# Loading V in one transfer, and U and V behind the first batch's last chunk

## The chip, the cores and the metric

The kernel runs on one core of one Trainium2 chip. The metric is the device time of one execution in microseconds (us); lower is better. The times of the kernel before are three executions.

## What is computed

For each of 4 batches and 8 heads, 768 positions of width 48 go through a recurrent attention; its result `x` (768 x 384 for each batch) goes through a low-rank mixing over the positions and a two-layer MLP:

```
for t in range(S):
    cur = einsum('bhd,bhe->bhde', u[None] * kt, vt)
    y[:, :, t] = einsum('bhd,bhde->bhe', rt, state + cur)
    state = w[None, :, :, None] * state + einsum('bhd,bhe->bhde', kt, vt)
...
h = xt @ U @ V                      # U is 768 x 32, V is 32 x 768
u = x + h.transpose(0, 2, 1)
out = u + maximum(u @ w_ch1, 0) @ w_ch2     # 384 -> 1536 -> 384
```

U, V and the MLP's weights arrive as 64-bit floats. The kernel reads them as pairs of 32-bit integers and makes 32-bit floats of them on ScalarE and VectorE.

## The kernel before, in words

Each batch is cut into 6 chunks of 128 positions (`NCH`). For a chunk `n` three tensors are loaded (`a_load`, L732: k, r and v, in this order, 192 KB each in 1,024 rows of 192 bytes). The first batch's chunks 0 to 5 make up the front of the kernel. In the front GpSimd (POOL) makes three products of each chunk (`a_ks`, L783 and L786; `a_dv`, L798; `a_dv_u`, L811), VectorE (DVE) reduces the last one (`a_dg`, L818), scales and copies the transposed r (`a_tr`, L858), masks the scores (`a_am`, L1018), adds states (L1059) and forms `x` (`a_x`, L1027). TensorE (PE) transposes k and r (L849), makes scores (L881), state updates (L895), and the chunk's output (`a_visit`, L914 and L918). ScalarE (ACT) scales v (L822) and decays the state (L1067).

U is used in `g_product` (L1132): for each chunk six matmuls multiply its `x` by U. V is spread to three copies on partitions by a selection matrix `sel` (`v_split`: four matmuls for each half, seen as L414 writing `pab`), and its high and low parts are kept in `V3` (L670, L671). When all six chunks have their product, `c_g` writes `Gs` (L1156 to L1164), `c_xu` adds V times `Gs` to the transposed `x`, and the first batch's MLP begins. PE then works through the MLP of one batch after another, with the attention of the next batch woven in. All matmuls of the helper `whole` carry line 414.

Every operation is first recorded with a key. A planner in the kernel (`Plan.schedule`) goes through them with costs of its own, gives each to an engine, and writes one fixed order for each engine; the engines then take their instructions strictly in that order. Of the operations that an engine could begin, the smaller key goes first. A product or subtraction that either engine can do (`on_either`) goes to POOL or to DVE, and DVE and POOL take turns in those that use their shared port; the planner writes these turns down as waits. A load has a planned landing time (`LANDS`, and `late` for each load). SyncE's queue (SP) issues nearly all loads.

The keys that matter here: chunk `n` of the front loads at `-90 + n`, so chunk 4 at -86 and chunk 5 at -85. U's load has key -86.5 and V's -85.5. U's conversion has key 16 (`U_CONV`), V's 30.05 (`LATER`), chunk c's output `9 + 4.2 * c`. The first four MLP weights load behind the third chunk's scores in the plan, which for SP is only a place in the order.

```
at(t_load, load)         # U: -86.5, V: -85.5
for n in range(1, NCH):
    at(-90 + n, lambda n=n: a_load(n))
```

So SP issues: chunks 0 to 3, U, chunk 4, V in four parts, chunk 5, weights. The parts of V are the four column blocks of 192 columns: part c fills partitions 32c to 32c + 31.

Of the kernel before, what the change touches and what calls it, by code (L numbers as in the profile page):

```python
# [341 lines left out]
def dve(n):  # L342
    return 130 + 1.09 * n


def act(n):
    return 285 + 0.6 * n
# [7 lines left out]
def rwkv_moe(ctx: ExitStack, tc: tile.TileContext, r, k, v, w, u, U, V, w1, w2, out):  # L355
# [11 lines left out]
    R = U.shape[1]  # L367
# [26 lines left out]
    def wbuf(shape, dt, tag, bufs, name):  # L394
        return Buf(work, shape, dt, tag, bufs, name)
# [7 lines left out]
    def bank(tag, name):  # L403
        if tag in lasting:
            return lasting[tag]
        return Buf(ps, [128, 512], F32, tag, {"acc": 3}.get(tag, 1), name)

    def f32(ap):
        return ap.bitcast(F32)


    def whole(*args, **kw):

        return nc.tensor.matmul(*args, **kw)  # L414
# [7 lines left out]
    def on_act(n, fn, w_, r_, times=1, dk=0.0):  # L422
        return op("ACT", times * (act(n) - 94) + 94, fn, w_, r_, dk=dk)

    def on_either(n, fn, w_, r_, dk=0.0, only=None):

        ways = [("POOL", pool(n), lambda: fn(nc.gpsimd), True), ("DVE", dve(n), lambda: fn(nc.vector), True)]
        return one_of(ways, w_, r_, only, dk)
# [5 lines left out]
    def dma(fn, w_, r_, rows, run, eng="SP", ns=470, dk=0.0, late=0.0, either=False):  # L434

        q = nc.scalar if eng == "ACT" else nc.sync
        return op(eng, ns, lambda: fn(q), w_, r_, dma=rows * max(0.96 if run >= 500 else 1.18 if run == 192 else 1.3, run / 366),
                  rows=rows, late=late, dk=dk, alt=[("ACT", ns, lambda: fn(nc.scalar), False)] if either else ())
# [9 lines left out]
    ident_ = const.tile([128, 128], F32, name="ident")  # L448
# [27 lines left out]
    sel = wbuf([128, 3 * 128], F32, "xh", NXS, "sel")  # L476
# [87 lines left out]
    def big(shape, dt, name):  # L564
        return xbuf(shape, dt, "big", NBIG, name)
# [6 lines left out]
    def unit(name, shape, parts, split):  # L572

        P_ = shape[0]
        n = 1
        for s_ in shape[1:]:
            n *= s_
        raw = big([128, 2 * n], I32, f"raw_{name}") if wide else big([128, n], F32, f"raw_{name}")

        def view(ap):  # L580
            return ap if len(shape) == 2 else ap.rearrange("p (a c) -> p a c", a=shape[1])

        loaded = [(raw, i) for i in range(len(parts))]

        def load(mark=None):
            big_one = len(parts) == 1 and name != "u"
            before = landing[-FLYING] if big_one and len(landing) >= FLYING else None
            mine = []
            if big_one:
                landing.append((mine, Buf(const, [1, 1], F32, None, 1, f"landed_{name}")))  # L590
            for i, (p0, ap) in enumerate(parts):
                runs = 1 if len(ap.shape) == 2 else ap.shape[1]

                def start(q, p0=p0, ap=ap):
                    mine.append(q.dma_start(view(raw.t[p0:p0 + ap.shape[0]]), ap.bitcast(I32) if wide else ap))  # L595
                    if before:
                        tc.add_manual_dep(mine[0].ins, before[0][0].ins.name,
                                          mybir.DependencyInfo(mybir.DependencyClass.Sync, mybir.DependencyReason.DATA),
                                          reason="no more of them at a time")
                dma(start, [(raw, i)] + ([landing[-1][1]] if big_one else []), ([before[1]] if before else []) + ([mark] if mark else []),  # L600
                    ap.shape[0] * runs, (8 if wide else 4) * n // runs, ns=370, late=LATE + 1500 * (name == "v") + SLACK * (big_one and len(landing) <= 2 * EARLY))

        def word(i):
            return raw.t[:P_].rearrange("p (n two) -> p two n", two=2)[:, i]

        def byte():
            return raw.t[:P_].bitcast(U8).rearrange("p (n e) -> p n e", e=8)[:, :, 3]

        def fl():
            return view(word(0).bitcast(F32) if wide else raw.t[:P_])  # L610

        def on_dve_byte():
            return nc.vector.tensor_scalar(word(0), byte(), 2.0 ** -5, 7.0, ALU.mult, ALU.min)

        def on_act_byte():

            nc.scalar.activation(word(0), byte(), AF.Copy, scale=7.49 / 255)  # L620

        def sign():
            return nc.vector.scalar_tensor_tensor(word(0), word(1), -2 ** 31, word(0), ALU.bitwise_and, ALU.bitwise_or)

        def join():
            return nc.vector.scalar_tensor_tensor(word(0), word(1), 3, word(0), ALU.logical_shift_left, ALU.bitwise_or)  # L626

        def convert():
            if wide:
                op("DVE", 100 + 0.65 * n, on_dve_byte, [(raw, "lo")], loaded, lock=True,  # L630
                   alt=[("ACT", act(n) + 100, on_act_byte, False)])
            if wide:
                on_act(n, lambda: nc.scalar.activation(word(1).bitcast(F32), word(1).bitcast(F32), AF.Copy,  # L633
                                                       scale=2.0 ** -112), [(raw, "hi")], loaded)
                mark = [pool_done] if name in ALONE else []
                op("DVE", dve(n), sign, [(raw, "lo")], [(raw, "hi")] + mark, lock=True)
                op("DVE", dve(n), join, [(raw, "lo")], [(raw, "hi")], lock=True)
            split(fl, raw)
        return load, convert

    def weight_units():
        units = []

        def split_to(d, key, name):
            t = d[key] = big([128, 2, DM], F32R, name)

            def go(fl, raw):
                def to(i):
                    return t.t[:, i] if len(fl().shape) == 2 else t.t[:, i].rearrange("p (c n) -> p c n", c=NCT)
                on_act(384, lambda: nc.scalar.copy(to(0), fl()), [(t, 0)], [raw])  # L650
                on_either(384, lambda e: e.tensor_tensor(to(1), fl(), f32(to(0)), ALU.subtract), [(t, 1)],  # L651
                          [raw, (t, 0)], only=None)
            return go

        def u_split(fl, raw):
            on_act(192, lambda: nc.scalar.copy(Uf.t, fl()), [Uf], [raw])

        def v_split(fl, raw):
            for j in range(S // DM):
                pt = bank(("tr", "sc")[j], f"pv_{j}")  # L660

                def spread(j=j, pt=pt):
                    for i in range(DM // NV):
                        c = j * (DM // NV) + i
                        whole(pt.t[:3 * R, i * NV:(i + 1) * NV],
                              lhsT=sel.t[:, c * 3 * R:(c + 1) * 3 * R], rhs=fl(),
                              start=(i == 0), stop=(i == DM // NV - 1), skip_group_check=True)
                sl = slice(j * DM, (j + 1) * DM)
                pe(715, spread, [pt], [raw, sel], k=4)
                on_act(384, lambda sl=sl, pt=pt: nc.scalar.copy(V3.t[:, sl], pt.t[:3 * R, :DM]), [(V3, j)], [pt])  # L670
                on_dve(384, lambda e, sl=sl, pt=pt: e.tensor_tensor(V3.t[2 * R:, sl], pt.t[2 * R:3 * R, :DM],  # L671
                                                                    f32(V3.t[2 * R:, sl]), ALU.subtract), [(V3, j)], [pt])

        units.append(unit("u", [128, NCH, R], [(0, U.rearrange("(c p) r -> p c r", p=128))], u_split))
        NV = S * R // 128
        units.append(unit("v", [128, NV], [(c * R, V[:, c * NV:(c + 1) * NV]) for c in range(128 // R)], v_split))
        for f in range(NFT):
            fs = slice(f * 128, (f + 1) * 128)
            units.append(unit(f"w1_{f}", [128, NCT, 128], [(0, w1[:, fs].rearrange("(c p) n -> p c n", p=128))],
                              split_to(W1, f, f"w1s_{f}")))  # L680
            units.append(unit(f"w2_{f}", [128, DM], [(0, w2[fs, :])], split_to(W2, f, f"w2s_{f}")))
        return units
# [805 lines left out]

    T0, PER = 45.0, 1.98
    START = 1  # L1490
    U_LOAD, V_LOAD, U_CONV = -86.5, -85.5, 16
    LATER = 30.05
    SPLIT, HOLD = 5, 2
    GXD = 4
# [18 lines left out]
    for _ in range(START):  # L1513
# [2 lines left out]
    at(-99, lambda: a_load(0))  # L1516
    at(-98, lambda: on_act(384, lambda: nc.scalar.copy(
        sel.t.rearrange("p (c k r) -> p c k r", k=3, r=R),
        ident_.rearrange("p (c r) -> p c r", r=R).unsqueeze(2).broadcast_to([128, 128 // R, 3, R])), [sel], []))
    at(UB, load_u)  # L1520
    at(-97, lambda: urgent(tables))
    for n in range(1, NCH):
# [145 lines left out]
```

## Time and profile before

| what | us |
|---|---|
| median of three executions | 405.62 |
| lowest and highest | 405.07, 406.38 |
| span of the profiled execution | 406.6 |
| start of the first batch's MLP matmuls in it | 44.55 |
| start of the last stores in it | 401.06 |

The profiled execution has no timed value of its own beside its span of 406.6 us, which lies 1.0 us above the median and 0.2 us above the highest of the three. Times inside the profile are microseconds from the first instruction. A row that names an engine with a small q (SPq) is that engine's queue issuing a transfer. In the chain of work that ended last, each row is the start, the length and what ran. The figure in square brackets behind a row of the timeline is the engine's idle time before it and what ended it.

### The profile page before, as it was taken

To read this page: it belongs to the slowest core of one execution; us is meant where nothing else is said; L and a number is where in the kernel's file an instruction comes from. 1 tells how busy PE (TensorE), PEld (TensorE's weight loads), DVE (VectorE), ACT (ScalarE), POOL (GpSimd) and SP (SyncE) were. 2 spreads that over 40 slices of the span, in tenths; PEclk is the share of its full clock that TensorE was granted. 3 is DMA by queue.
4 is the path that set the end of the run, shared out by engine and by line. 5 is a ranking of instruction groups with operands and counts; after the bars stand their busy time and mean duration, and the time that the engine had idled before them with its cause. 6 is when DMAs were issued, how large, how long until landed. Compare 5 with 4: busy or idle time off the path is not lost.

```text
span 406.6 us, 11920 instructions
## 1 busy us (share of the span) xinstructions
PE 394.2 (97%) x4928; PEld 376.1 (92%) x4928; DVE 274.8 (68%) x615; ACT 177.2 (44%) x432; POOL 65.4 (16%) x86
## 2 busy tenths in 40 slices
PE   8997999999999999999999999999999999999994
PEld 5876899999998999999999999999999999999993
DVE  7868889999999979789647678898515261221122
ACT  2795859673786324223324242222224243223320
POOL 2960120233523302011003100010001000000000
PEclk9998999999999999999999999999999999999999
DMA  9969797968967765686667755782200520001001
GB/s 143 168 153 240 139 252 154 255 111 164 260 123 146 168 168 82 117 154 127 126 108 134 145 117 78 134 155 62 60 2 2 117 60 0 2 0 58 2 0 65
DMA packets 195741, 46.27 MB, mean 114 GB/s; under 512 B 179422, under 2 KB 194144, under 8 KB 195680
## 3 DMA queue, kind: packets, MB, share of 16 engines
q1 hardware_dynamic: 194352, 44.85, 55.2%
q8 instruction: 40, 0.66, 0.7%
q10 hardware_dynamic: 1328, 0.59, 0.5%
q14 instruction: 21, 0.17, 0.1%
HBM read 37.16 MB, written 8.26 MB: 112 GB/s over the span
## 4 chain that ended last, share of the span: by engine, by line
PE 75%; SPq 8%; DMA 5%; issue 4%; DVE 3%; POOL 2%; ACT 1%; DVEq 0%; POOLq 0%
PE p L414 64%; SPq L732 4%; PE pab L881 3%; SPq L771 2%; PE pav L932 2%; SPq L595 2%; PE pav L937 2%; PE pab L895 1%; DMA ub<-ud 1%; PE pab L414 1%; DMA ldr<-in_r_dram 1%; DMA ldv<-in_v_dram 1%; DMA vsw<-in_v_dram 1%; PE pav L914 1%; PE pav L918 1%
## 5 line engine op out<-in xcount | busy, mean ns | idle before, releaser
L414 PE MATMUL p<-uTh,w1s 128*128 128x384 f32 x576 | 147.6, 337 | 0.0
L1321 ACT ACTIVATE hr<-p 128x384 f32<-128x384 f32 x96 | 47.1, 491 | 178.0 <-PE p L414 173.7
L414 PE MATMUL p<-w2s,hh 128*128 128x384 f32 x576 | 119.6, 338 | 0.1
L1323 DVE TENSOR_TENSOR hl<-hr,hh 128x384 fp32r<-128x384 f32 x83 | 46.1, 555 | 102.3 <-ACT hh L1322 99.9
L414 PEld LDWEIGHTS p<-uTh,w1s 128*128 128x128 f32 x576 | 103.5, 188 | 0.9 <-DVE w1s L651 0.3
L414 PEld LDWEIGHTS p<-w2s,hh 128*128 128x128 f32 x576 | 100.7, 188 | 1.4 <-POOL w2s L651 0.4
L414 PE MATMUL p<-uTl,w1s 128*128 128x384 f32 x288 | 96.2, 335 | 0.0
L414 PE MATMUL p<-w2s,hl 128*128 128x384 f32 x288 | 66.7, 335 | 0.0
L414 PEld LDWEIGHTS p<-uTl,w1s 128*128 128x128 f32 x288 | 54.0, 188 | 0.1
L414 PEld LDWEIGHTS p<-w2s,hl 128*128 128x128 f32 x288 | 51.3, 188 | 0.2
L1322 ACT CAST hh<-hr 128x384 fp32r<-128x384 f32 x96 | 49.2, 512 | 2.5
L822 ACT ACTIVATE dv<-ldv,dg 128x48 f32<-128x48 f32 x96 | 23.1, 322 | 6.6 <-DVE dg L818 6.5
L1323 POOL TENSOR_TENSOR hl<-hr,hh 128x384 fp32r<-128x384 f32 x13 | 13.2, 1016 | 64.0 <-PE pav L937 36.7
L1095 POOL TENSOR_TENSOR SW<-S,wm 112x192 f32<-112x192 f32 x13 | 6.6, 508 | 93.2 <-DVE S L1086 87.8
L881 PEld LDWEIGHTS pab<-rT,kT 48*64 48x64 f32 x768 | 13.6, 134 | 7.7 <-issue 3.0
L1018 DVE TENSOR_TENSOR am<-pab,mask 128x256 f32<-128x256 f32 x48 | 19.1, 413 | 1.2 <-PE pab L881 1.1
L881 PE MATMUL pab<-rT,kT 48*64 48x64 f32 x768 | 16.9, 224 | 2.4 <-DVE rT L858 2.4
L1027 DVE TENSOR_TENSOR x<-pav,dv 128x384 f32<-128x384 f32 x24 | 13.1, 548 | 6.7 <-PE pav L937 5.2
L1361 DVE TENSOR_TENSOR x<-p,x 128x384 f32<-128x384 f32 x33 | 16.3, 548 | 1.0 <-PE p L414 1.0
L818 DVE TENSOR_REDUCE dg<-dv 128x8 f32<-128x384 f32 x24 | 13.0, 540 | 2.4 <-POOL dv L811 2.3
L626 DVE SCALAR_TENSOR_TENSOR raw_w<-raw_w 128x384 int32<-128x384 int32 x24 | 13.0, 549 | 0.1
L633 ACT ACTIVATE raw_w<-raw_w 128x384 f32<-128x384 f32 x24 | 13.0, 556 | 0.0
(178 smaller groups left out, 503.0 us busy)
## 6 DMA issues: line engine op xcount, KB each, us to landing
raw_w<-in_moe_w_ch_dram SPq DMA_DIRECT2D x24, 384.0 KB, 5.0
ldv<-in_v_dram SPq DMA_DIRECT2D x24, 192.0 KB, 3.9
ldk<-in_k_dram SPq DMA_DIRECT2D x20, 192.0 KB, 4.4
ldr<-in_r_dram SPq DMA_DIRECT2D x20, 192.0 KB, 4.0
bl<-in_r_dram SPq DMA_DIRECT2D x79, 48.0 KB, 3.1
bl<-in_k_dram SPq DMA_DIRECT2D x79, 48.0 KB, 2.4
ud<-x SPq DMA_DIRECT2D x18, 192.0 KB, 3.2
ub<-ud SPq DMA_DIRECT2D x18, 192.0 KB, 3.6
```

What stands on the lines that cost most here:

```text
L414: return nc.tensor.matmul(*args, **kw)
L626: return nc.vector.scalar_tensor_tensor(word(0), word(1), 3, word(0), ALU.logical_shift_left, ALU.bitwise_or)
L633: on_act(n, lambda: nc.scalar.activation(word(1).bitcast(F32), word(1).bitcast(F32), AF.Copy, scale=2.0 ** -112), [(raw, "hi")], loaded)
L732: dma(lambda q, i=i, src=src: q.dma_start(part(i)[:, :, :D], src[b, :, c * C:(c + 1) * C, :].rearrange("h p d -> p h d")), [ts[i]] if n < ...
L822: nc.scalar.activation(dv.t[:, h], v_of(n, h), AF.Copy, scale=dg.t[:, h:h + 1])
L881: return nc.tensor.matmul(pt.t[o * C2:(o + 1) * C2, q * C2:(q + 1) * C2], lhsT=kT.t[rows, q, i * C2:(i + 1) * C2], rhs=rT.t[rows, q, i * C ...
L1018: on_dve(256, lambda e: e.tensor_tensor(am.t, abs_[n][j].t[:, :SU].rearrange("p (h t) -> p h t", h=NP), mask_.unsqueeze(1).broadcast_to([1 ...
L1027: nc.vector.tensor_tensor(x.t[:, c0:c1], pav[0].t[:, c0:c1], dv.t.rearrange("p h d -> p (h d)")[:, c0:c1], ALU.add)
L1321: on_act(384, lambda: nc.scalar.activation(hr.t, pt.t[:, :TB], AF.Relu), [hr], [pt])
L1322: on_act(384, lambda: nc.scalar.copy(hh.t, hr.t), [hh], [hr])
L1323: on_either(384, lambda e: e.tensor_tensor(hl.t, hr.t, f32(hh.t), ALU.subtract), [hl], [hr, hh], only=None)
L1361: on_dve(384, lambda e, x=x, pt=pt: e.tensor_tensor(x.t, pt.t[:, :DM], x.t, ALU.add), [x], [pt])
```

## The change

V's load becomes one transfer of 128 rows of 1,536 bytes. Row r of V (of 32) is cut in four, and its pieces lie on partitions 4r to 4r + 3; `sel` is arranged to match. The condition that keeps U and V out of the limit on weight loads in flight is reworded for the single part. The keys of both loads move behind chunk 5's: U to -84.6 and V to -84.5. SP's order becomes: chunks 0 to 3, chunk 4, chunk 5, U, V, weights.

```diff
         def load(mark=None):
-            big_one = len(parts) == 1 and name != "u"
+            big_one = name not in ("u", "v")
...
-        units.append(unit("v", [128, NV], [(c * R, V[:, c * NV:(c + 1) * NV]) for c in range(128 // R)], v_split))
+        units.append(unit("v", [128, NV], [(0, V.rearrange("r (c n) -> (r c) n", n=NV))], v_split))
...
-    U_LOAD, V_LOAD, U_CONV = -86.5, -85.5, 16
+    U_LOAD, V_LOAD, U_CONV = -84.6, -84.5, 16
...
-        ident_.rearrange("p (c r) -> p c r", r=R).unsqueeze(2).broadcast_to([128, 128 // R, 3, R])), [sel], []))
+        ident_.rearrange("p (r c) -> p c r", r=R).unsqueeze(2).broadcast_to([128, 128 // R, 3, R])), [sel], []))
```

## Rows read from the trace of the kernel before

**Rows 1.** Busy time by long stretches: PE, PEld, DVE, ACT, POOL, clock, DMA share, GB/s.

```profile
0.00:44.00 44.00, 38.33 (x780) 30.69 (x781) 35.55 (x97) 27.44 (x95) 19.64 (x33) 0.96 0.96 178
44.00:131.00 87.00, 86.40 (x1203) 82.21 (x1202) 81.97 (x185) 61.25 (x154) 23.64 (x27) 1.00 0.82 178
131.00:401.00 270.00, 269.49 (x2946) 263.17 (x2946) 156.76 (x335) 88.48 (x184) 22.13 (x27) 1.00 0.43 83
```

**Rows 2.** Chain that ended last, from chunk 5's load to the last product.

```profile
23.72 4.34 DMA ldr<-in_r_dram
28.19 1.00 POOL dv L798
...
33.45 1.58 PE pav L914 x31
35.03 1.48 PE pav L918 x16
...
37.02 0.85 PE pab L414 x4
37.87 1.06 PE pav L914 x32
38.94 0.81 PE pav L918 x16
...
40.60 0.60 PE wake L1132 x12
```

**Rows 3.** Timeline of SP's queue: start, length, transfer issued.

```profile
10.45 1.33 SPq L732 DMA_DIRECT2D ld<-in_r_dram  x1
...
12.89 2.46 SPq L595 DMA_DIRECT2D raw_u<-in_moe_U_dram  x1
...
17.89 4.09 SPq L595 DMA_DIRECT2D raw_v<-in_moe_V_dram  x4
22.02 1.65 SPq L732 DMA_DIRECT2D ldk<-in_k_dram  x1
23.72 0.59 SPq L732 DMA_DIRECT2D ldr<-in_r_dram  x1
...
25.11 3.93 SPq L595 DMA_DIRECT2D raw_w<-in_moe_w_ch_dram  x4
```

**Rows 4.** The columns of rows 1, by single microseconds.

```profile
19.00:20.00 1.00, 1.00 (x49) 0.95 (x41) 1.00 (x4) 1.00 (x6) 0.92 (x2) 1.00 0.89 177
...
23.00:24.00 1.00, 1.00 (x70) 0.94 (x68) 0.93 (x3) 1.00 (x5) 0.92 (x2) 1.00 0.05 8
```

**Rows 5.** Timeline of POOL.

```profile
22.76 1.01 POOL L798 TENSOR_TENSOR dv<-ldr,ldk 128x384 f32<-128x384 f32 x1 [0.92 <-ACT SW L1067]
...
26.28 1.02 POOL L786 TENSOR_TENSOR ks<-ldk,tab 128x384 f32<-128x384 f32 x1 [1.42 <-DMA ldk<-in_k_dram]
28.19 1.00 POOL L798 TENSOR_TENSOR dv<-ldr,ldk 128x384 f32<-128x384 f32 x1 [0.90 <-DMA ldr<-in_r_dram]
...
29.30 1.00 POOL L811 TENSOR_TENSOR dv<-dv,ub 128x384 f32<-128x384 f32 x1
```

**Rows 6.** Timeline of DVE.

```profile
22.26 0.36 DVE L626 SCALAR_TENSOR_TENSOR raw_u<-raw_u 128x192 int32<-128x192 int32 x1
...
30.33 0.55 DVE L818 TENSOR_REDUCE dg<-dv 128x8 f32<-128x384 f32 x1 [2.33 <-POOL dv L811]
...
36.55 0.56 DVE L1027 TENSOR_TENSOR x<-pav,dv 128x384 f32<-128x384 f32 x1 [0.88 <-PE pav L918]
```

**Rows 7.** Timeline of PE, narrowed to 32 to 48 us.

```profile
32.75 0.69 PE L881 MATMUL pab<-rT,kT 48*64 48x64 f32 x32 [2.38 <-DVE rT L858]
```

**Rows 8.** The columns of rows 1, two microseconds with the clock down.

```profile
34.00:36.00 2.00, 2.00 (x34) 1.91 (x33) 1.67 (x6) 0.65 (x2) 0.00 (x0) 0.50 1.03 187
```

**Rows 9.** Tile ld (chunks 0 to 3): its loads' time from issue to landing.

```profile
DMA to landing us min/median/max: 3.0/4.9/6.2
```

**Rows 10.** Tile raw_u: its load's time to landing.

```profile
DMA to landing us min/median/max: 5.2/5.2/5.2
```

**Rows 11.** Timeline of ACT: U's first and last conversion.

```profile
20.53 0.37 ACT L620 ACTIVATE raw_u<-raw_u 128x192 int32<-128x192 uint8 x1
...
23.06 0.36 ACT L656 COPY Uf<-raw_u 128x192 f32<-128x192 f32 x1
```

**Rows 12.** Timeline of PE, where the second batch's MLP begins.

```profile
131.10 0.44 PE L414 MATMUL pab<-V,Gs 96*128 96x384 f32 x1 [0.53 <-DVE xT L1235]
```

## The prediction

> **What bounds the kernel now.** I read the busy times by long stretches first [rows 1]. After 44 us TensorE is busy 86.40 of 87.00 us and then 269.49 of 270.00 us; behind the front the kernel is a stream of matmuls with no holes worth counting. In the front, 0 to 44 us, it is busy only 38.33 us, and its mean clock is 0.96. So a change in the front is worth what it takes off the moment when the first batch's MLP can begin, if what the stream needs later keeps up.
>
> The chain of work that ended last says what sets that moment [rows 2]. It goes through SP's queue of loads to the r of chunk 5, issued at 23.72 and landed 4.34 us later, then through POOL's `dv` at 28.19, and on through TensorE's outputs of chunks 4 and 5, the spreading of V (the row at 37.02) and the last two products with U (12 matmuls at 40.60). The queue's timeline shows why that r comes so late [rows 3]: U's issue at 12.89 holds the queue 2.46 us, V's four parts at 17.89 hold it 4.09 us, and only then come chunk 5's k at 22.02 and its r. Nor do the DMA engines use this time: their share is 0.89 between 19 and 20 us and 0.05 between 23 and 24 [rows 4]. The queue is not waiting for bandwidth there; little has been given to the engines.
>
> Then the waits, engine by engine. POOL waits 1.42 us for chunk 5's k and 0.90 us for its r [rows 5]. VectorE's next instruction in order is the reduction of that chunk's `dv`, so VectorE stands still 2.33 us, until 30.33 [rows 6]. Behind it in VectorE's order stand chunk 4's masks and chunk 5's rT, and TensorE stands 2.38 us until rT is there at 32.75 [rows 7]. After this stop the granted clock falls: it is 0.50, the 1.2 GHz level, from 34 to 36 us [rows 8]. So one late load is paid for three times: on POOL, on VectorE with TensorE behind it, and in the clock.
>
> **Part 1: chunk 5's loads before U and V.** U's 2.46 us and V's 4.09 us no longer stand ahead of them. From 12.89 the queue now issues six chunk tensors. Their rows go from 0.59 us (chunk 5's r) to 1.33 us (chunk 3's r) [rows 3]; with the longest for each, k starts at 12.89 + 3 x 1.33 = 16.9 and r at 18.2; with the longest landing of the chunk loads, 6.2 us [rows 9], they are there by 23.1 and 24.4. POOL would then work without its waits. The first of them, 0.92 us before chunk 4's `dv` at 22.76, is put down to ScalarE, but VectorE's conversion of U ran from 22.26 to 22.62 just ahead of it [rows 5, 6], and the two engines take turns; with U's conversion elsewhere it goes too. Without all three (0.92 + 1.42 + 0.90 = 3.24 us) the last product, which ends at 30.30 now, ends at 27.06. k is wanted at 26.28 - 0.92 - 1.42 = 23.94 and r one product later, at 24.95: both are there even with the long figures.
>
> VectorE was idle from 28.00 (30.33 - 2.33), so a last product at 27.06 takes the whole 2.33 us away, with 0.94 us to spare. If U's conversion again falls between two POOL products, that costs 0.92 us of these 0.94 and still nothing. What is late next is then VectorE itself. I take **-2.33 us**.
>
> **Part 2: the clock.** Without a stop of 2.38 us I expect the clock to stay at its upper level, as it did in the 30 us before. Chunk 4's output, partly at the lower level, takes 1.58 + 1.48 = 3.06 us on the chain; the same work for chunk 5 takes 1.06 + 0.81 = 1.87 us at the upper one [rows 2]. I take **-1.19 us**; the bounds are 0 (a stop still long enough) and 1.19.
>
> **Part 3: U later.** Its load starts six tensors after 12.89: at 16.4 with the short figure, at 20.9 with the long one. Landing took 5.2 us [rows 10], at most 6.2 for a neighbour [rows 9]; U's conversions took from 20.53 to 23.42 [rows 11], 2.89 us. So U is ready between 24.5 and 30.0 us, instead of 23.42. The products with U of chunks 0 to 2, made by 30 us before, then fall later. Each is half of the row of 12 matmuls, 0.30 us [rows 2]. If TensorE waits for others anyway they cost 0; if they all fall on its chain, 0.90. TensorE will still have short waits for VectorE, but I don't know where the planner puts them; I take the middle, **+0.45 us**.
>
> The conversions are not more work, only later work. On VectorE they are two instructions of 0.36 us [rows 6]; taken out ahead of 28 us and put in behind it, they cost at worst 0.72 us on the chain to rT and give at best 0.72 us. I take 0 and keep both ends.
>
> The rows alone say that U is ready by 30.0 us and that the first thing on the new chain, chunk 5's scores, starts at 32.75 - 2.33 = 30.4. Here the Trainium skill speaks against the change: the page DMA: Bandwidth & Descriptors, section Rules for kernel authors, says to issue a DMA early and to wait for it late, and U's load is issued later and waited for sooner. By that rule the saving of part 1 would be paid back as a wait for U; by the rows 0.4 us is left even with the long figures, and the sum keeps its 2.33.
>
> **Part 4: V in one transfer and later.** V's four issues take 4.09 us, and their shortest bound in one piece is a chunk tensor's, 0.59 us. V's load would start at the latest at 20.9 + 2.46 = 23.4, and if the single issue took all of 4.09 us and 6.2 us to land after that, it would be there at 33.7. It is spread at 37.02 now [rows 2], at about 33.5 when 3.5 us earlier, and VectorE and ScalarE convert it before. So only the very worst of both figures would show. At the middle figures it lands near 27. I cost it at 0. The weights behind it start at 25.11 now [rows 3]; they would start at about 22 with a one-issue V, and at 27.5 at worst, with four weights to convert after that which are not wanted before 38. Also 0. `sel` is only arranged another way: 0.
>
> **The sum at `Gs`.** -2.33 - 1.19 + 0.45 = -3.07 us.
>
> **Part 5: does it reach the end?** From 44 to 131 us VectorE is busy 81.97 of 87.00 us [rows 1]; it prepares the second batch while TensorE does the first batch's MLP, and at 131.10 TensorE waits 0.53 us for VectorE's xT [rows 12]. There is no slack at that place, so the gain that reaches the end is the smaller of TensorE's and VectorE's. VectorE gets 2.33 us earlier for certain, and also its 0.88 us wait for the slow chunk 4 output at 36.55 [rows 6] if the clock stays up: 2.33 to 3.21, middle 2.77. I take **-2.8 us**. The profiled execution would be 406.6 - 2.8 = 403.8 us; the median of the three runs was 1.0 us below that span, 405.62, so I forecast **402.8 us**. The forecast's own range: with U's products and conversions all on the chain 2.33 + 1.19 - 0.90 - 0.72 = 1.90; with the conversions' 0.72 as a gift and nothing for the products 4.24. That is 401.4 to 403.7.
>
> **Rivals.**
>
> *Half of it.* Something else takes VectorE's wait over. ScalarE is the candidate: it is busy the whole of both microseconds of [rows 4]. Against it: U's and V's conversions also ran on it then, and move out of its way. If half of the 2.33 stays as a wait and the clock still falls, -1.17 + 0.45 = -0.7, so about 404.9; mixtures lie between 403.7 and 405.0. Chance 0.18.
>
> *Nothing at the end.* The second batch's preparation is bound by its own loads and turns, which do not move with the front; TensorE arrives early at 131.10 and waits. For it: the 0.53 us there. Against it: VectorE is nearly full all the way, so its 2.33 us should carry. 405.6, within 0.3% (1.2 us, about what a measurement of this kernel can tell from no change). Chance 0.12.
>
> *Slower: the planner moves work from POOL to VectorE.* All orders are planned anew. POOL did 27 instructions between 44 and 131 us [rows 1], most of them products that VectorE could do at 0.56 us each, like the one at 36.55 [rows 6]. With VectorE nearly full and no slack at 131.10, each one moved costs 0.56. Five undo the forecast, eight make it more than 1.2 us slower; at ten, 405.6 - 2.8 + 5.6 = 408.4. For it: the place has no slack. Against it: VectorE has less to catch up, so nothing pushes the planner there. Chance 0.13.
>
> *U or V late.* TensorE stands at the first product with U. It decides when U is ready after 30.4 + 2.8 = 33.2, that is when it lands after 30.3, over 9 us after its latest start; the longest landing in the rows is 6.2. This is what the page's rule would make of it: 405.6 or a little more. Chance 0.03.
>
> *More than forecast,* below 401.4, if VectorE also meets shorter waits in the second batch: 0.04. The forecast has 0.50.
>
> **Numbers.** Faster by over 1.2 us, that is under 404.4: 0.50 + 0.04 + about 0.11 of the half case = 0.65. Within: 0.07 + 0.12 + 0.02 = 0.21. Slower: 0.13 + 0.01 = 0.14. The range 401.3 to 406.5 leaves out the 0.04 below and the 0.14 above.
>
> **What would show it.** Right: chunk 5's k issued at 15 to 17 us and no long dip of the DMA share before 20; POOL without waits for k and r; no VectorE wait of 2 us at the reduction; TensorE's stop before chunk 5's scores under half a us and the clock at 1.00 from 32 to 36; the first MLP matmuls at about 41.5 instead of 44.55; and no new TensorE wait of over 1 us at the second batch's start. Wrong: TensorE waiting for `Uf` or for V's spreading, a VectorE wait elsewhere in the front, the clock still falling, or a stop before the second batch that eats the gain.

## The result and the profile after

The changed kernel takes 408.55 us (median of 20 executions, 406.94 to 411.24), the kernel before 405.91 us (20, 404.70 to 410.84). The ratio is 1.0062, 95% interval 1.0044 to 1.0081: **slower by 0.6%, about 2.5 us**, where 402.8 us was forecast. The profiled execution of after has a span of 409.5 us and took 411.24 us, so the time is the span and 1.7 us more. By that the execution of before that the prediction was read from (span 406.6) took about 408.3 us, 2.7 us above the median of the three runs, and not 1.0 us as the prediction had it: it was one of the long ones (5 of the 20 timed executions of before lie above 407 us).

What the front does with its loads is close to the forecast. SP's queue in after (start, length, transfer; answers to [rows 3]):

```profile
13.05 2.31 SPq L732 DMA_DIRECT2D ldk<-in_k_dram  x1
...
17.01 1.03 SPq L732 DMA_DIRECT2D ldk<-in_k_dram  x1
18.08 2.40 SPq L732 DMA_DIRECT2D ldr<-in_r_dram  x1
...
21.18 0.89 SPq L595 DMA_DIRECT2D raw_u<-in_moe_U_dram  x1
22.12 0.54 SPq L595 DMA_DIRECT2D raw_v<-in_moe_V_dram  x1
```

Chunk 5's k and r are issued 5.0 and 5.6 us earlier. But the two holds of the queue of over 2 us are still there, at 13 and at 18 us: now chunk 4's k and chunk 5's r stand in them, where [rows 3] have U and V (2.39 us of V's 4.09 us is its first part). The holds are not made by U and V; only V's three further issues are gone.

POOL's last product and VectorE's reduction of it in after (answers to [rows 5, 6]; the bracket is the idle time ahead of the row):

```profile
26.07 1.00 POOL L811 TENSOR_TENSOR dv<-dv,ub 128x384 f32<-128x384 f32 x1
```

```profile
27.11 0.55 DVE L818 TENSOR_REDUCE dg<-dv 128x8 f32<-128x384 f32 x1 [1.07 <-POOL dv L811]
...
32.09 0.56 DVE L1059 TENSOR_TENSOR S<-pav,SW 112x384 f32<-112x384 f32 x1 [1.07 <-ACT SW L1067]
```

POOL no longer waits and ends at 27.07. Yet TensorE stops ahead of the last chunks and again before the second batch's MLP:

```profile
31.32 0.49 PE L895 MATMUL pav<-ldv,ks 64*48 64x48 f32 x13 [1.35 <-DVE raw_v L616]
...
130.75 0.45 PE L414 MATMUL p<-uTh,w1s 128*128 128x384 f32 x1 [1.46 <-ACT hr L1321]
```

And by windows (columns of [rows 1]; they answer to [rows 1, 8]):

```profile
34.00:36.00 2.00, 2.00 (x28) 1.68 (x27) 0.48 (x3) 1.00 (x3) 0.00 (x0) 0.50 0.79 224
```

```profile
0.00:44.00 44.00, 39.88 (x780) 32.63 (x780) 34.79 (x96) 28.39 (x96) 19.57 (x33) 0.92 0.97 185
44.00:131.00 87.00, 84.23 (x1188) 79.80 (x1188) 80.83 (x184) 59.98 (x152) 23.47 (x26) 1.00 0.78 169
```

The first MLP matmul is at 44.70 us (before: 44.55), so in these two executions the front is even. The stream behind it has lost 2.17 us of TensorE's busy time between 44 and 131 us (84.23 against 86.40). The place to look is thus behind the front; my first reading still looked in the front.

### The profile page after: what moved, and what is told of

Same layout as the page of the kernel before. It is cut to its first block, busy times and chain, and to the rows that moved or that the text cites. A ratio compares the mean times of both kernels' runs of the same rounds, so it can differ in the third digit from the quotient of the medians.

```text
span 409.5 us, 11917 instructions
## 1 busy us (share of the span) xinstructions
PE 396.5 (97%) x4928; PEld 377.9 (92%) x4928; DVE 272.4 (67%) x610; ACT 183.2 (45%) x457; POOL 67.1 (16%) x87
## 4 chain that ended last, share of the span: by engine, by line
PE 76%; DVE 8%; POOL 5%; SPq 4%; DMA 3%; issue 1%; ACT 1%; DVEq 0%; POOLq 0%; ACTq 0%
PE p L414 65%; SPq L771 3%; PE pab L881 2%; DMA ldk<-in_k_dram 1%; PE pav L932 1%; POOL dv L798 1%; POOL dv L811 1%; PE pab L414 1%; PE pav L937 1%; DMA raw_w<-in_moe_w_ch_dram 1%; PE pab L895 1%; DVE hl L1323 1%; DVE raw_w L623 1%; POOL ks L786 1%; POOL ks L783 1%
## 5 line engine op out<-in xcount | busy, mean ns | idle before, releaser
L1323 DVE TENSOR_TENSOR hl<-hr,hh 128x384 fp32r<-128x384 f32 x89 | 49.5, 556 | 106.6 <-ACT hh L1322 102.9
L822 ACT ACTIVATE dv<-ldv,dg 128x48 f32<-128x48 f32 x120 | 28.8, 322 | 5.5 <-DVE dg L818 5.5
L1323 POOL TENSOR_TENSOR hl<-hr,hh 128x384 fp32r<-128x384 f32 x7 | 7.1, 1017 | 62.1 <-PE pav L937 40.2
L811 POOL TENSOR_TENSOR dv<-dv,ub 128x384 f32<-128x384 f32 x12 | 12.1, 1012 | 18.1 <-DVE hl L1323 10.2
```

The source lines that it names most:

```text
L811: on_either(384, lambda e: e.tensor_mul(dv.t, dv.t, ub.t), [dv] + ([pool_done] if n == NCH - 1 else []), [ub], only="POOL" if front(n) els ...
L822: nc.scalar.activation(dv.t[:, h], v_of(n, h), AF.Copy, scale=dg.t[:, h:h + 1])
L1323: on_either(384, lambda e: e.tensor_tensor(hl.t, hr.t, f32(hh.t), ALU.subtract), [hl], [hr, hh], only=None)
```

## The experiments

In all tables "to MLP" is the start of the first `p<-uTh,w1s` matmul, and "MLP to 145" is from there to the same `p<-Gs,V` product near 145 us, both of one profiled execution: two executions of the same kernel differ in them by 2.43 and 0.34 us (before) and by 2.14 and 0.85 us (after). Where "to MLP" is 43.86 or more, and in `e_umoved`, the granted clock fell in the front. Each ratio is against runs of before on the same chip; their medians go from 405.91 to 406.90 us, so the times of two kernels are compared by their ratios. "Orders" are those that the planner wrote for the engines.

| kernel | orders: front / behind | us (runs) | ratio, 95% interval | to MLP | MLP to 145 |
|---|---|---|---|---|---|
| before, as predicted from | before / before | | | 44.55 | 100.46 |
| `e_before_again` | before / before | 405.83 (1) | | 42.12 | 100.80 |
| `e_same_v` | before, V moved / before | 406.75 (12) | 1.0003 (0.9976 to 1.0029) | 43.80 | 100.38 |
| `e_same_v_late` | same, V converted later / before | 405.81 (12) | 0.9990 (0.9966 to 1.0013) | 41.42 | 101.15 |
| `e_same_uv` | before, U and V moved / before | 411.77 (6) | 1.0109 (1.0073 to 1.0144) | 47.65 | 101.45 |
| `e_after_front` | after / before | 406.07 (12) | 0.9993 (0.9971 to 1.0014) | 42.12 | 100.88 |
| after | after / after | 408.55 (20) | 1.0062 (1.0044 to 1.0081) | 44.70 | 103.36 |
| `e_after_again` | after / after | 407.81 (1) | | 42.56 | 102.51 |
| `e_after_back` | after, old loads / after | 409.33 (12) | 1.0045 (1.0021 to 1.0069) | 43.55 | 102.91 |
| `e_before_front` | before / after | 410.43 (7) | 1.0091 (1.0059 to 1.0123) | 45.27 | 102.29 |
| `e_su_first` | own / own | 406.75 (12) | 1.0002 (0.9973 to 1.0031) | 42.22 | 100.84 |
| `e_vmoved` | own / own | 410.74 (4) | 1.0127 (1.0106 to 1.0148) | 43.86 | 103.79 |
| `e_one` | own / own | 408.58 (12) | 1.0056 (1.0028 to 1.0085) | 41.56 | 103.88 |
| `e_umoved` | own / own | 409.38 (6) | 1.0074 (1.0045 to 1.0103) | 43.56 | 100.28 |

**Loads and orders apart (`e_same_v`, `e_same_uv`, `e_after_back`, `e_su_first`).** My theory then was a local one: with U's products gone from ahead of it, TensorE's new order takes chunk 3's output and chunk 4's scores before chunk 4's state updates, VectorE's states come 2.5 us late (29.24 against 26.79), and the front loses what the loads had won.

`e_same_v` keeps before's orders and moves only V's load, as one transfer:

```diff
         self.schedule()
+        for i, o in enumerate(at["raw_v"]):
+            o.start = at["ldv_5"][0].start + 0.1 * (i + 1)
...
+                    if name == "v":
+                        if p0 == 96:
+                            whole_v = V.rearrange("r (c n) -> (r c) n", n=NV)
+                            q.dma_start(raw.t, whole_v.bitcast(I32) if wide else whole_v)
+                        return
```

`start` is a piece's place in the written orders. Three of V's four planned loads issue nothing, the last issues the whole.

> Every engine keeps the order of the kernel before; only V's load changes: one transfer, issued behind chunk 5's loads. U stays where it was. Theory (the loads' new places are a gain, the new order of the engines takes it back): chunk 5's r lands about 4 us earlier, VectorE's wait of 2.33 us at chunk 5's reduction is under 0.5, the clock stays up, the first MLP matmul is 2 to 3 us earlier than in the kernel before, and at least 2 us of it reach the end: about 403.5 us against 405.9. Rival (the loads set nothing; the second batch's preparation sets the end): 405.9, with a new TensorE wait of 2 us or more before 131 us.

406.75 us, where before has 406.90 on that chip: no difference. ScalarE's timeline in it (its lines are 12 to 14 further down) shows who took the wait over:

```profile
27.44 0.39 ACT L632 ACTIVATE raw_v<-raw_v 128x192 int32<-128x192 uint8 x1 [2.38 <-DMA raw_v<-in_moe_V_dram]
27.72 0.36 ACT L645 ACTIVATE raw_v<-raw_v 128x192 f32<-128x192 f32 x1
27.98 1.16 ACT L1081 ACTIVATE SW<-S,wm 112x96 f32<-112x96 f32 x4
```

The conversion of V stands ahead of SW of chunk 4 (the decayed state, which VectorE adds to), and VectorE then waits 2.64 us for SW. The prediction looked at when V is spread, not at when V is first read.

`e_same_uv` moves U as well, in before's orders:

```diff
+        for i, o in enumerate([at[f"ld{x}_{n}"][0] for n in (4, 5) for x in "krv"]):
+            o.start = u.start - 1 + 0.1 * i
+        for i, o in enumerate(at["raw_v"]):
+            o.start = u.start + 0.1 * (i + 1)
```

> Every engine keeps the order of the kernel before; U's and V's loads are issued behind chunk 5's, V in one transfer, as in the changed kernel. U's conversion thus stands in ScalarE's order where it stood at 20.5 us, and its data land near 26. Theory (U late is a price by itself in the old order, which the planner in the changed kernel avoids by moving the conversion): ScalarE stands 4 to 6 us, the first MLP matmul is 1 to 4 us later than in the kernel before, about 408 us. Rival (the order alone is to blame and U's lateness costs nothing): about 403 us.

411.77 us, more than the 408 us or so that were expected. ScalarE stands 5.23 us for U (lines 15 further down):

```profile
26.01 0.37 ACT L635 ACTIVATE raw_u<-raw_u 128x192 int32<-128x192 uint8 x1 [5.23 <-DMA raw_u<-in_moe_U_dram]
```

So the later U does need another order, and after's planner gave it one: there ScalarE converts U at 26.75 us without waiting.

`e_after_back` has after's orders, but issues U and V where before does:

```diff
+        at["raw_u"][0].start = at["ldk_4"][0].start - 0.5
+        at["raw_v"][0].start = at["ldk_5"][0].start - 0.5
```

> Every engine keeps the order of the changed kernel; only U's and V's loads are issued where the kernel before has them (U ahead of chunk 4's, V, in one transfer, ahead of chunk 5's). Theory (the new order of the engines costs the time): no faster than the changed kernel by more than 1 us, so 407.5 to 410 us, with chunk 4's added states as late as in the changed kernel. Rival (the places of the loads cost the time): at or below 406 us.

409.33 us: the loads back at their old places don't bring the time back. That points at the orders; which part of them, this run doesn't say.

`e_su_first` makes the planner put chunk 4's state updates (`su`) ahead of chunk 3's output:

```diff
+    first_ = Buf(const, [1, 1], F32, None, 1, "first_")
...
-        pe(530, lambda: in_turn(*both), pst[:2 if n < NCH - 1 else 1], ...
+        pe(530, lambda: in_turn(*both), pst[:2 if n < NCH - 1 else 1] + ([first_] if n == 4 else []), ...
...
+            own += [first_] if n == 3 else []
```

> The changed kernel with one more rule for the planner: chunk 4's state updates stand ahead of chunk 3's output in TensorE's order, as they did before the change. Theory (this one exchange delays the chain of states by 2.5 us): VectorE's chunk 4 states are ready 2 us or more earlier than in the changed kernel, the stop of 1.35 us before chunk 5's updates goes, and the time falls by 1 to 2.5 us, to 406 to 407.5. Rival (U's late conversion and products set the front, wherever the updates stand): the first MLP matmul within 0.5 us of the changed kernel's 44.70 and the time within 0.7 us of 408.5.

406.75 us, level with before, and at first I took that for proof of the local theory. It is none: the marker lets the planner write all later orders anew too, and the last column shows that the part behind the front became short again (100.84).

**A second profile of each kernel, and V alone moved.** `e_same_v_late` is `e_same_v` with V's conversions on ScalarE behind SW of chunk 5:

```diff
+        sw = [o for o in self.ops if any(b.name == "SW_5" for b in o.bufs) and o.eng == "ACT"][0]
+        late = [o for o in self.ops if o.eng == "ACT" and o.bufs[0].name == "raw_v"]
+        for i, o in enumerate(late):
+            o.start = sw.start + 0.1 * (i + 1)
```

> As the run with V in one transfer behind chunk 5 in the old order of engines (406.75 us), but ScalarE's conversion of V, in which it stood 2.38 us at 27.4 us for V's landing, stands behind SW of chunk 5. Theory (the gain of the earlier chunk loads was taken back by ScalarE's wait for V, which stands ahead of SW of chunk 4): VectorE's wait of 2.64 us for SW goes, its rT of chunk 5 comes about 2 us earlier than 31.89, the first MLP matmul by 1 to 2 us more, about 42.3, and the time falls to about 404.5 to 405.5. Rival 1 (something else is late next at the same place, such as the spreading of V, which needs the conversion): first MLP matmul at 43.5 or later, 406.5 to 407. Rival 2 (the front gains but the stream behind it gives it back before 139 us): first MLP matmul at 42.5 or earlier, and still 406 to 407.

VectorE's wait for SW shrinks from 2.64 to 0.33 us and its rT of chunk 5 comes at 29.52 instead of 31.89, as the theory said; the MLP begins at 41.42. But the time is 405.81 us, a ratio of 0.9990: not told from no change. What can be gained at this place at all is seen by comparing it with a second profile of before.

> Before once more, for a second profile. If its wait of 2.33 us on VectorE for the dv of chunk 5 and the drop of the clock to 0.50 are the kernel's, both are there again and the span is near 406; if they belong to the one execution that the prediction was read from, the wait is under 1.5 us or the clock stays at 1.00 between 32 and 38 us, and the first MLP matmul comes 1 us or more ahead of 44.55.

SP's queue, VectorE and a window in it (answers to [rows 3, 6, 8]):

```profile
22.06 0.42 SPq L732 DMA_DIRECT2D ldk<-in_k_dram  x1
22.53 0.58 SPq L732 DMA_DIRECT2D ldr<-in_r_dram  x1
```

```profile
29.03 0.55 DVE L818 TENSOR_REDUCE dg<-dv 128x8 f32<-128x384 f32 x1 [0.31 <-POOL dv L811]
```

```profile
34.00:36.00 2.00, 2.00 (x38) 1.41 (x36) 1.97 (x6) 1.06 (x4) 0.00 (x0) 1.00 0.80 216
```

Here the 2.33 us wait of [rows 6] is 0.31, the clock stays at 1.00, and the MLP begins at 42.12, 2.43 us earlier than in the execution that I had read. Chunk 5's k took 1.65 us to issue there and takes 0.42 here. The stall was real, but it comes in some executions and not in others; this one's time, 405.83 us, lies near the median.

> After once more, for a second profile. If the lateness of chunk 4's states is the order's and not one execution's, S_4_0 begins at 29 us again, 2.4 us behind the 26.8 us of before, and the first MLP matmul stands at 44 to 45 us. If it was this execution's own, S_4_0 begins before 28 us.

The lateness of S_4_0, the first of chunk 4's states on VectorE, is there again (29.46), yet the MLP begins at 42.56 and not at 44 to 45, with the clock up, only 0.44 us behind `e_before_again`. Behind that place the two part. Waits of TensorE from 44 to 140 us (us in total, times, longest), first in `e_before_again`, then in `e_after_again`:

```profile
PE pab L414 <- DVE xT L1235: 0.6, 1, 0.6
PE pav L932 <- issue: 0.3, 1, 0.3
```

```profile
PE p L414 <- ACT hr L1321: 2.1, 2, 1.5
PE pab L414 <- DVE xT L1235: 0.2, 1, 0.2
```

At 145 us `e_after_again` is 2.15 us behind, and its span at the end 2.0 us longer: 0.44 from the front, 1.71 from between 42 and 145 us.

`e_vmoved` is after with U's load left at its old key:

```diff
-    U_LOAD, V_LOAD, U_CONV = -84.6, -84.5, 16
+    U_LOAD, V_LOAD, U_CONV = -86.5, -84.5, 16
```

> After, but with U's load left at its old place in the order of loads; V's one transfer stays behind chunk 5, and all is planned anew; in this plan TensorE keeps chunk 4's state updates ahead of chunk 3's output. Theory (the loss comes from U's move alone, by way of TensorE's order): no loss, 404.5 to 407, with VectorE's state instructions of chunk 4 before 28 us and the first MLP matmul before 44.2. Rival (the loss belongs to V's move or to the new plan of the stream as such): 408 to 409, as after.

410.74 us, slower than after, though VectorE's states of chunk 4 are early (26.85 and 27.51) as expected. My theory fell here: the order that I had blamed is as in before, and the loss is larger. It is made between the MLP's start and 145 us (103.79).

**The cross.** That left the orders behind the front. When the planned first MLP matmul begins, the same 300 pieces of work are done in both plans (by my count one more in before, two more in after), so the two halves can be exchanged. `e_after_front` takes after up to there, and from there before's places and engines, from a written table (`STREAM`, not shown); `e_before_front` does the reverse, with V in four parts at its old place.

```diff
         self.schedule()
+        for row in STREAM.split():
+            n, start, way = row.split(":")
+            o = self.ops[int(n)]
+            o.start = float(start)
+            o.eng, _, o.fn, o.locks = o.ways[int(way)]
```

> After's orders up to the first MLP matmul, and from there the orders and engines that before has, work for work (the same 300 pieces of work stand ahead of that place in both). In two executions whose clock stayed up, after came 0.43 us later than before to the first MLP matmul (42.56 against 42.12) and 2.16 us later to the place past 145 us. Theory A (the larger part of the loss is made behind the front, by the new interleaving of the second batch's preparation with the stream): the holes at 96 and 126 us go, the lag past 145 us is 0.3 to 0.7 us, and the time is 406.3 to 407. Theory B (the front's lateness is passed on and grows, whatever the order behind it): holes of 1 us or more stay before 132 us, and the time is 407.8 to 408.8, as after.

> The counterpart: before's orders and loads up to the first MLP matmul, V in four parts, and from there after's orders and engines. Theory A: the holes of after behind the front are there though nothing of the change is, 407.5 to 408.3. Theory B: no such holes, 405.8 to 406.5, as before.

406.07 and 410.43 us, one 0.2 us below and the other 2.1 us above what theory A had. The whole change with before's order behind the front is level with before; before's own front with after's order behind it is no faster than after. TensorE's waits from 44 to 140 us, in `e_after_front` and in `e_before_front` (lines 5 further down):

```profile
PE pab L419 <- DVE xT L1240: 0.6, 1, 0.6
```

```profile
PE p L419 <- ACT hr L1326: 1.5, 1, 1.5
PE pu L419 <- DVE Gs L1169: 0.6, 1, 0.6
PE p L419 <- issue: 0.3, 1, 0.3
PE pab L419 <- DVE xT L1240: 0.2, 1, 0.2
```

The hole at ScalarE's hr goes with the order, not with the loads. The profiled `e_before_front` also has the stall of the execution of before that I had read: a VectorE wait of 2.01 us for chunk 5's `dv`, and a mean clock of 0.92 in the front. So of the 4.7 us between its span (408.8) and that of `e_before_again` (404.1), 3.15 stand ahead of the MLP and 1.49 between there and 145 us: the order costs 1.49 us in this profile, and why the seven executions lie as high as 410.43 isn't shown. What carries the finding is `e_after_front`, with the interval 0.9971 to 1.0014 against 1.0044 to 1.0081 for after.

`e_one` (V in one transfer, nothing moved) and `e_umoved` (that and U moved) are the other parts alone, planned anew. Their edits of after:

```diff
-    U_LOAD, V_LOAD, U_CONV = -84.6, -84.5, 16
+    U_LOAD, V_LOAD, U_CONV = -86.5, -85.5, 16
```

```diff
-    U_LOAD, V_LOAD, U_CONV = -84.6, -84.5, 16
+    U_LOAD, V_LOAD, U_CONV = -84.6, -85.5, 16
```

> V in one transfer alone, both loads at their old places, all planned anew. Theory A (what the time shows is chiefly the draw of the new plan behind the front): the front is within 0.5 us of the 42.12 us of before, and the time follows from new holes between 75 and 135 us; here the plan is near that of the run with V moved alone, so 409.5 to 411. Rival (one transfer instead of four is by itself harmless): 405.5 to 406.5.

> After with V's one transfer at its old place and U's load behind chunk 5, all planned anew. Theory of the first runs (U's move puts chunk 3's output ahead of chunk 4's state updates, and that is the loss): 408 to 409, as after. Theory A: the front is within 0.7 us of 42.12, the rest is what the new plan behind it makes, between 405.5 and 409, and it is the sum of the holes between 75 and 135 us.

`e_one`, 408.58 us, lies 0.9 us below theory A's range and is still the clearest case: its front is the second earliest of all (41.56), and it loses 3.1 us behind it (103.88 against 100.80). `e_umoved` speaks against theory A: it is slow (409.38, above the range) with no holes behind the front (100.28). Its front is 1.44 us late (the clock is at 0.57 from 32 to 34 us), and in its profile 7.8 us pass from SP's last store to the end, where the other kernels have 5.6 to 6.1. Why, stays open.

## Why the prediction was wrong

**Part 1, its mechanism.** Right: k at 17.01 (16.9 forecast), r at 18.08 (18.2), POOL without waits, its last product ended at 27.07 (27.06). That k and r fit so closely is partly luck: the sum had no hold in it, and the one of 2.31 us took the place of issues that were shorter than the 1.33 us of the sum (0.63 and 0.90). Nor was 1.33 us the longest: [rows 3] have 1.65 us for chunk 5's k, with which k and r would be there by 24.0 and 25.7, later than wanted (23.94 and 24.95). Two things were wrong. U and V were blamed for holds of the queue that stay when they are gone. And the size, -2.33 us, was read off a stall of one execution; in the second profile of before the same wait is 0.31. It comes and goes with the front's own loads: r of chunk 5 was issued at 23.72 in the first, at 22.53 in the second, and at 23.46 in `e_before_front`, which has the same front and a wait of 2.01. What chunk 5's earlier loads and a later V are worth without the stall can be estimated from `e_same_v_late` against `e_before_again`, one profile each: 0.70 us at the MLP's start, 0.35 at 145 us.

**Part 2.** The clock fell in the profiled after (0.50 in the window shown) and didn't in `e_after_again`, with nearly the same stop of TensorE (1.35 and 1.40 us). In `e_after_back` it stayed at 1.00 after a stop of 2.08 us. The -1.19 us came from the same one execution as the -2.33: priced at 3.52 us together, where the MLP's starts of the two executions of before lie 2.43 us apart.

**Part 3.** U's load began at 21.18 us, just past the bound of 20.9, and its last conversion ended at 29.06, inside the range for U. The +0.45 us looks like what the front lost between the two later profiles (0.44), but `e_after_front`, with the same order up to there, reached the MLP at 42.12, as early as before. So no loss in the front is shown, and the late states of chunk 4 cost nothing that can be seen at the MLP's start. The Trainium skill's advice to issue a DMA early and wait late (DMA: Bandwidth & Descriptors, Rules for kernel authors) is borne out where the orders stay: 5.23 us of waiting for U in `e_same_uv`. Replanned, after doesn't show that wait.

**Part 4.** V's 0 fits after, where no engine is seen waiting for V's landing, since the planner moved V's conversion; in the old order V cost ScalarE 2.38 us (`e_same_v`). In after, the row of TensorE's stop of 1.35 us names a conversion of V on VectorE as what ended it; no run tests that.

**Part 5, the step that failed.** It carried the front's gain to the end as if the work behind the front kept its order, and took the gain off a median near which the stall isn't seen (`e_before_again`). The miss of 5.75 us (408.55 against 402.8) is thus two things: the forecast gain of 2.8 us (0.7%) was not there (`e_after_front`, with everything of the change but the new order behind the front, has a ratio of 0.9993, interval 0.9971 to 1.0014), and the new order behind the front cost some 2.5 us. The prediction says itself that all orders are planned anew, and priced that as a rival, with POOL's work going to VectorE. The place was right and the way wrong. Windows from 44 to 139 us, of `e_before_again` and then `e_after_again`:

```profile
44.00:139.00 95.00, 94.01 (x1245) 89.71 (x1244) 89.48 (x201) 63.25 (x157) 27.95 (x31) 1.00 0.82 178
```

```profile
44.00:139.00 95.00, 92.68 (x1235) 88.16 (x1234) 89.01 (x200) 64.48 (x164) 28.37 (x31) 1.00 0.82 174
```

POOL has 31 instructions in both and VectorE about as many (201 and 200); nothing was moved from one to the other in sum. What differs is who stands behind whom. ScalarE ahead of the largest hole, in `e_after_again` and then in `e_before_again`:

```profile
125.70 0.54 ACT L650 CAST w2s<-raw_w 128x384 fp32r<-128x384 f32 x1 [0.58 <-DVE raw_w L626]
126.72 0.51 ACT L1181 CAST Gs<-gf 32x384 fp32r<-32x384 f32 x1 [0.48 <-DVE gf L1175]
127.26 0.49 ACT L1321 ACTIVATE hr<-p 128x384 f32<-128x384 f32 x1
```

```profile
124.94 0.51 ACT L1181 CAST Gs<-gf 32x384 fp32r<-32x384 f32 x1
125.48 0.51 ACT L1184 CAST Gs<-gf 32x384 fp32r<-32x384 f32 x1
126.02 0.49 ACT L1321 ACTIVATE hr<-p 128x384 f32<-128x384 f32 x1
```

TensorE in the same two profiles (the products with U and with w2, and in the first the last matmul ahead of the hole and the one behind it):

```profile
121.73 1.20 PE L414 MATMUL p<-w2s,hh 128*128 128x384 f32 x6
...
123.38 1.20 PE L1132 MATMUL pab<-x,Uf 128*32 128x96 f32 x48
...
126.01 0.34 PE L414 MATMUL p<-uTl,w1s 128*128 128x384 f32 x1
127.80 0.62 PE L414 MATMUL p<-uTh,w1s 128*128 128x384 f32 x2 [1.45 <-ACT hr L1321]
```

```profile
120.95 1.20 PE L1132 MATMUL pab<-x,Uf 128*32 128x96 f32 x48
122.08 1.31 PE L414 MATMUL p<-w2s,hh 128*128 128x384 f32 x6
...
125.31 1.20 PE L414 MATMUL p<-w2s,hh 128*128 128x384 f32 x6
```

In after (`e_after_again`) the second batch's products with U come 2.43 us later, behind the products with w2 at 121.73 instead of ahead of those at 122.08; `gf` and `Gs` follow late, and hr, which frees the accumulator that TensorE wants next, stands behind the first `Gs` on ScalarE. TensorE's last product ahead of the hole ended at 126.35, hr began at 127.26, so 0.91 of the 1.45 us is hr's place on ScalarE, and the rest is hr itself. In before hr stands behind `Gs` too (126.02), but there TensorE has the products with w2 at 125.31 to do meanwhile; in after it has done them before. This chain is read from the trace; putting hr ahead of `Gs` by hand was not tried. That the new order behind the front makes the loss is shown by `e_after_front`; that this chain is the reason is not.

The test that the prediction named, "no new TensorE wait of over 1 us at the second batch's start", would have found it. A loss by the new order, whatever it moves, belonged among the rivals with a larger chance than 0.13: of the five kernels with a plan of their own (after among them) four are slower than before and none is faster.

## What to carry to other kernels

When a planner or compiler orders everything anew, a small edit is two changes: itself, and a new draw of all orders. Cost them apart, and test them apart by crossing the old order with the new part; here the part (`e_after_front`) was worth nothing that could be measured, and the draw cost 2.5 us. Before a stall is priced from one profile, see that the profiled execution's time is near the median, in the same measure: span with span or time with time.

## What the runs showed of the hardware that was not expected

SP's queue has two holds of 2.0 to 3.2 us at about 12 to 13 and 17 to 18 us in every profile, whatever transfer stands there: U and V's first part in before (2.46, 2.39), chunk 4's k and chunk 5's r in after (2.31, 2.40), two loads of v in `e_same_v_late` (2.33 at 11.88, 2.15 at 16.76). The same order of loads has them at other transfers in another execution: `e_before_front` issues as before does, and there they are at v of chunks 3 and 4 (2.39 at 11.92, 3.21 at 16.61). What makes them is open.

The same program's front has a mean granted clock of 0.92 in one execution and 1.00 in another (after and `e_after_again`), after stops of TensorE that differ by 0.05 us (1.35 and 1.40). In `e_after_back` TensorE stopped for 2.08 us at 28.4 us, and the clock stayed at 1.00.
